# A depthwise convolution and a gated feed-forward layer on one core: the convolution's band built in four groups, the first feature block taken chunk by chunk, the last projection evicted in three parts

## The chip, the cores and the metric

The kernel runs on one core of a Trainium2 chip. The core's engines run side by side, each through its own queue in order: TensorE (PE, matmuls; its weight loads are a row of their own, PEld), VectorE (DVE), ScalarE (ACT), GpSimd (POOL) and SyncE (SP). They wait for each other through semaphores. Transfers go through 16 DMA engines, and are issued from the queues of SP, ACT or POOL. The metric is the device time of one execution in microseconds (us), the median over runs: 775.72 us before the change (three runs, 775.3 to 775.95).

## The reference

Eight sequences of 4096 tokens with 192 features go through a causal depthwise convolution of 7 taps, whose weights are a softmax over the taps and belong to 8 heads of 24 features. Its output, 32768 tokens, goes through a feed-forward layer of 1536 features with a ReLU gate.

```python
w = weight - np.max(weight, axis=-1, keepdims=True)
w = np.exp(w)
w = w / (np.sum(w, axis=-1, keepdims=True) + 1e-09)
x_pad = np.concatenate([np.zeros((B, pad, D), dtype=np.float32), x], axis=1)
idx = np.arange(S)[:, None] + np.arange(K)[None, :]
x_unf = x_pad[:, idx, :].reshape(B, S, K, H, group)
out = np.einsum('hk,bskhg->bshg', w, x_unf)
...
gate = np.maximum(x @ w_gate, 0.0)
val = x @ w_val
return (gate * val @ w_out).astype(np.float32)
```

Inputs and output are float32; the kernel computes its matmuls on float16 operands.

## The kernel before

**Units.** The work is cut into 16 units of 1024 tokens (`UNIT`) of two sequences at a time, four sequences apart. Features lie on partitions in three chunks of 64 (`NCH`); the two sequences take the lower and the upper 64 partitions of one tile, so that two matmuls with 64 rows run side by side. `Wg` and `Wv` are loaded into the lower half by GpSimd's queue and copied into the upper half, columns in five pieces (`CUTS`, 128, 256, 384, 384 and 384 columns); DVE copies the first two pieces, GpSimd the rest (L164).

**One unit.** `gate_val` runs twice (windows of 512 tokens), each with 12 blocks of 128 gate features. A block is six matmuls with `Wg` into one tile of PSUM and six with `Wv` into another (L441), a ReLU on ACT (L451, it reads the gate tile) and a product on DVE (L452, it reads the value tile). PSUM is a pool of four such tiles used in rotation, so a block's value tile is needed again by the value matmuls two blocks later. Then `project` runs four times (window by sequence): 48 matmuls with `Wo` in four quarters of 128 tokens (L459), one ACT copy of 768 columns into `out_s` (L467), and one store of 384 KB issued by SP. There are three `out_s` buffers.

**Convolution.** From unit 2 on it is done elementwise for the unit after the next: ACT, DVE and GpSimd share the products and sums per tap (`lane_first`, `lane_rest`, `product`, `add`), on x that was turned round by transposing transfers. For units 0 and 1 there is no time for this, and TensorE does it: a matmul with a band matrix, 118 rows (112 tokens and 6 before them) by 112 columns, for each head. `conv_dense(0)` and `conv_dense(1)` make window 0 and window 1 of unit 0, each 120 small matmuls (L274) in three channel chunks, each chunk followed by a cast into `xc` (chunk 1 on DVE, the others on ACT, L284). `conv_dense(0)` stands before the first gate block, `conv_dense(1)` after eight blocks. `conv(2)` and `conv(3)` make unit 1, during unit 0's projection.

**The opening.** Before the band exists, the tap weights come in (L110), replicated over 64 partitions in each half: four heads on partitions 0 to 63, four on 64 to 127. DVE and ACT make the softmax (L179 to L188). GpSimd makes `eye`, an identity pattern of 64 rows in each half (L137). DVE multiplies it with the taps (`prod`, L220: 4 heads x 32 columns x 7 taps = 896 elements a partition) and sums over the taps (`blk`, L228). The result holds a 64 by 32 block of each head's band. Copies on DVE (L237, six) and ACT (L239, four) put it at its places in the two band tiles, which were zeroed. Meanwhile TensorE runs 18 matmuls on zeros (L125), and three more after `conv_dense(0)` (L478). GpSimd's queue in the opening: x loads for `conv_dense(0)`, the two selections for `eye`, eight weight loads, x loads for `conv_dense(1)`, weight copies and loads, `late` and the x loads for `conv(2)`, weight copies.

**Order.** The order on each engine is written out by hand (`manual_schedule`); a queue does not overtake. In units 0 to 13 ACT's products for the unit after the next stand ahead of the four projections, in groups of four. In unit 0 only eleven of them do, and the three for the last tap run in unit 1, ahead of blocks 4, 8 and 12 of its 24.

Of the kernel before, what the change touches and what calls it, by code (L numbers as in the profile page):

```python
# [8 lines left out]
FP = mybir.dt.float32  # L9
F16 = mybir.dt.float16  # L10
# [5 lines left out]
def kernel(  # L16
# [12 lines left out]
    nc = tc.nc  # L29

    B, S, D = x.shape
    H, KW = weight.shape
    G = D // H
    DFF = moe_w_gate.shape[1]
    PAD = KW - 1
    NB = B // 2
    NCH = D // 64
    NBLK = D // 32
    NFF = DFF // 128
    WIN = 512  # L40
    NWIN = S // WIN
    SUB = 112
# [8 lines left out]
    NUNIT = NB * S // UNIT  # L51
# [9 lines left out]
    const = ctx.enter_context(tc.tile_pool(name="const", bufs=1))  # L61
# [42 lines left out]
    xts = {}  # L104
    xts[0] = load_x(0)

    HH = H // 2
    wr = const.tile([128, HH, KW], FP)
    for half, eng in ((0, nc.sync), (1, nc.scalar)):
        eng.dma_start(  # L110
            out=wr[64 * half : 64 * half + 64],
            in_=bass.AP(
                tensor=weight.tensor,
                offset=weight.offset + half * HH * KW,
                ap=[[0, 64], [KW, HH], [1, KW]],
            ),
        )
    ones = const.tile([128, 32 + KW], FP)
    nc.vector.memset(ones[:], 1.0)

    zeros = const.tile([128, 512], F16)
    nc.vector.memset(zeros[:], 0.0)  # L122
    ps = psum.tile([128, 2, 512], FP, name="ps")
    for n in range(18):
        nc.tensor.matmul(  # L125
            out=ps[:, n % 2, :], lhsT=zeros[:, 0:128], rhs=zeros[:], start=True, stop=True
        )

    bands = [const.tile([128, HH, SUB], F16, name=f"band{half}") for half in range(2)]
    for half in range(2):  # L130
        nc.vector.memset(bands[half][:], 0.0)

    eye = const.tile([128, 32 + KW], FP)
    for half in range(2):
        nc.gpsimd.affine_select(  # L137
            out=eye[64 * half : 64 * half + 64],
            in_=ones[64 * half : 64 * half + 64],
            pattern=[[-1, 32 + KW]],  # L140
            compare_op=ALU.is_equal,
            fill=0.0,
            base=0,
            channel_multiplier=1,
        )

# [42 lines left out]
            out=e[:], in0=e[:], in1=sm[:].to_broadcast([128, n, KW]), op=ALU.mult  # L189
        )  # L190

    we = const.tile([128, HH, KW], FP)
    softmax(we, wr, HH)

    tap = const.tile([128, NCH, KW], FP)

    def load_taps():
        late = const.tile([128, HH, KW], FP)
        nc.gpsimd.tensor_copy(out=late[:], in_=we[:])
        for c in range(NCH):  # L200
            r0 = 0
            while r0 < 64:
                h = (64 * c + r0) // G
                r1 = min(64, G * (h + 1) - 64 * c)
                for half in range(2):
                    p0 = 64 * (h // HH)
                    nc.sync.dma_start(
                        out=tap[64 * half + r0 : 64 * half + r1, c, :],
                        in_=late[p0 : p0 + r1 - r0, h % HH, :],
                    )  # L210
                r0 = r1

# [1 line left out]
    xts[2] = load_x(2)  # L214
    pool_halves(4)

    prod = const.tile([128, HH, 32, KW], FP)
    e0 = eye[:, 0:1]
    w0 = we[:, 0:1, 0:1]
    nc.vector.tensor_tensor(  # L220
        out=prod[:],
        in0=bass.AP(tensor=e0.tensor, offset=e0.offset, ap=[e0.ap[0], [0, HH], [1, 32], [1, KW]]),
        in1=bass.AP(tensor=w0.tensor, offset=w0.offset, ap=[w0.ap[0], [KW, HH], [0, 32], [1, KW]]),
        op=ALU.mult,
    )
    blk = const.tile([128, HH, 32, 1], F16)
    with nc.allow_low_precision("one of the terms is not zero"):
        nc.vector.tensor_reduce(out=blk[:], in_=prod[:], axis=mybir.AxisListType.X, op=ALU.add)  # L228

    places = [(0, 0, 64, 0), (64, 0, 64, 64), (32, 0, 32, 32), (64, 32, 64, 32), (96, 0, 32, 96)]  # L230
    for half in range(2):
        for n, (r0, b0, b1, s0) in enumerate(places):
            ncol = min(32, SUB - s0)
            src = blk[64 * half + b0 : 64 * half + b1, :, 0:ncol, 0]
            dst = bands[half][r0 : r0 + b1 - b0, :, s0 : s0 + ncol]
            if n % 2 == 0:
                nc.vector.tensor_copy(out=dst, in_=src)  # L237
            else:
                nc.scalar.copy(out=dst, in_=src)  # L239

    def band(h):
        return bands[h // HH][0 : SUB + PAD, h % HH, :]

    xc = {}

# [138 lines left out]
    def product(engine, u, c, k):  # L384
        out = prods[u][:, k, c, :]
        in_, scale = shifted(u, c, k, 1), tap[:, c, k : k + 1]
        if engine is nc.scalar:
            engine.activation(out=out, in_=in_, func=ACTF.Copy, scale=scale)  # L388
        else:
            engine.tensor_scalar(out=out, in0=in_, scalar1=scale, scalar2=None, op0=ALU.mult)  # L390
# [37 lines left out]
    def gate_val(u, w):  # L428
        h = hpool.tile([128, NFF, 2, WIN], F16, name="hT")
        xcb = xc[u]  # L430
        for f in range(NFF):
            if u == 0 and w == 0 and f == 8:
                conv_dense(1)
            if u == 1 and w * NFF + f in (4, 8, 12):
                product(nc.scalar, u + 1, (w * NFF + f) // 4 - 1, KW - 1)
            pss = []
            for W in (Wg, Wv):
                ps = psum.tile([128, 2, 512], FP, name="ps")
                for c in range(NCH):
                    for st in range(2):  # L440
                        nc.tensor.matmul(  # L441
                            out=ps[:, st, :],
                            lhsT=W[64 * st : 64 * st + 64, c, 128 * f : 128 * (f + 1)],
                            rhs=xcb[64 * st : 64 * st + 64, c, WIN * w : WIN * (w + 1)],
                            start=(c == 0),
                            stop=(c == NCH - 1),
                            tile_position=(64 * st, 0),
                        )
                pss.append(ps)
            gr = gpool.tile([128, 2, WIN], F16, name="gr")  # L450
            nc.scalar.activation(out=gr[:], in_=pss[0][:], func=ACTF.Relu)  # L451
            nc.vector.tensor_tensor(out=h[:, f], in0=gr[:], in1=pss[1][:], op=ALU.mult)  # L452
        return h

    def project(bp, w, h, st):
        ps = psum.tile([128, 2, 512], FP, name="ps")
        for q in range(4):
            for f in range(NFF):
                nc.tensor.matmul(  # L459
                    out=ps[:, q // 2, D * (q % 2) : D * (q % 2) + D],  # L460
                    lhsT=h[:, f, st, 128 * q : 128 * (q + 1)],
                    rhs=Wo[:, f, :],
                    start=(f == 0),
                    stop=(f == NFF - 1),
                )
        os_ = opool.tile([128, 2, 2 * D], FP, name="out_s")
        nc.scalar.copy(out=os_[:], in_=ps[:, :, 0 : 2 * D])  # L467
        row0 = (bp + NB * st) * S + WIN * w
        nc.sync.dma_start(
            out=out[row0 : row0 + WIN, :].rearrange("(q p) d -> p q d", p=128),  # L470
            in_=os_[:].rearrange("p a (b d) -> p (a b) d", d=D),
        )


    conv_dense(0)
    ps = psum.tile([128, 2, 512], FP, name="ps")
    for n in range(3):
        nc.tensor.matmul(  # L478
            out=ps[:, n % 2, :], lhsT=zeros[:, 0:128], rhs=zeros[:], start=True, stop=True
        )  # L480
    lane_load(2)
    nc.gpsimd.dma_start(out=Wo[:], in_=moe_w_out.rearrange("(c p) d -> p c d", p=128))
    for u in range(NUNIT):
        lane = 1 <= u < NUNIT - 1
        if lane:
            add(u + 1, 1)
        if u == 1:
            lane_load(3)
            add(2, 2)
            add(2, 3)  # L490
        if u + 2 < NUNIT:
            lane_turn(u + 2)
        if u == 0:
            xts[3] = load_x(3)
        if 0 < u < NUNIT - 3:
            lane_load(u + 3)
        if lane:
            for k in range(4 if u == 1 else 2, KW - 1):
                add(u + 1, k)
        hs = [gate_val(u, w) for w in range(2)]  # L500
        if lane:
            add(u + 1, KW - 1)
        if u == 0:
            xc[1] = xcpool.tile([128, NCH, UNIT], F16, name="xc")
            conv(2)
        del xc[u]
        work = [[] for _ in range(4)]
        if u + 2 < NUNIT:
            lane_first(u + 2)
            lane_rest(u + 2)  # L510
            todo = [(c, k) for k in (0, 1, 2, 3, 4, 6) for c in range(NCH)]
            todo = [ck for ck in todo if ck not in VECTOR[u > 0] and (u or ck[1] < 6)]
            work = [todo[4 * i : 4 * i + 4] for i in range(4)]
        bp, w0 = u * UNIT // S, u * UNIT % S // WIN
        for i in range(4):
            for c, k in work[i]:
                product(nc.scalar, u + 2, c, k)
            project(bp, w0 + i // 2, hs[i // 2], i % 2)
            if u == 0 and i == 0:
                conv(3)  # L520

# [29 lines left out]
```

## Time and profile before

| what | us |
|---|---|
| median of three runs | 775.72 (775.3 to 775.95) |
| the profiled execution | 776.04 |
| its span on the core | 774.3 |
| TensorE matmuls busy | 767.1 (99%) |
| VectorE busy | 687.1 (89%) |
| ScalarE busy | 602.4 (78%) |
| GpSimd busy | 371.4 (48%) |
| first gate matmul starts | 10.86 |
| last projection matmul ends, by the chain | 769.80 |

The span is one profiled execution, from its first instruction to its last; the execution's own time is 1.7 us longer. The granted clock of TensorE is 1.0 throughout. Busy times of matmuls overlap, as they are pipelined; the chain of waits, followed back from the last instruction, says better what sets the end. Per block of gate and value work TensorE takes 1.295 us, per projection 4.0 us.

### The profile page before, as it was taken

The page shows a single profiled execution, that of the slowest core. Times are in us where ns is not written, and L with a number is a line of the kernel's source. Part 1 is how long each engine was busy: PE and PEld are TensorE (multiplying, and loading weights), DVE is VectorE, ACT ScalarE, POOL GpSimd, SP SyncE. Part 2 cuts the span into 40 slices and gives each one's busy share as a digit, 9 for nine tenths or more (in the row PEclk, how much of TensorE's full clock was granted, in tenths as well). Part 3 has the DMA queues.
Part 4 walks back from the last instruction along what each step waited for, and adds up shares of the span by engine and source line. Part 5 has one row for each costly group of instructions (what it writes and reads, how often), then busy time and mean ns, then how long its engine had stood idle before and what let it go on. Part 6 is the DMA issues. An engine that isn't in the chain of part 4 may idle for free.

```text
span 774.3 us, 19017 instructions
## 1 busy us (share of the span) xinstructions
PE 767.1 (99%) x7957; PEld 501.5 (65%) x7957; DVE 687.1 (89%) x733; ACT 602.4 (78%) x732; POOL 371.4 (48%) x213
## 2 busy tenths in 40 slices
PE   9999999999999999999999999999999999999997
PEld 4485584856748466484765848567484674847657
DVE  7889999989999899999999999899998999995590
ACT  5797887878778887787878878788787877875571
POOL 9606829084380935709266291743909346080000
PEclk9999999999999999999999999999999999999999
DMA  9957828171272813628153281622828021200102
GB/s 114 129 96 125 90 83 93 42 115 20 88 88 63 105 28 80 75 79 98 31 94 52 83 91 41 106 30 83 92 63 106 22 80 37 67 18 22 62 2 82
DMA packets 132565, 55.63 MB, mean 72 GB/s; under 512 B 98176, under 2 KB 132480, under 8 KB 132480
## 3 DMA queue, kind: packets, MB, share of 16 engines
q1 hardware_dynamic: 90592, 38.45, 24.3%
q0 software_dynamic: 41808, 15.97, 18.8%
q8 instruction: 62, 1.02, 0.6%
q14 instruction: 23, 0.19, 0.1%
q10 hardware_dynamic: 80, 0.01, 0.0%
HBM read 31.94 MB, written 25.17 MB: 74 GB/s over the span
## 4 chain that ended last, share of the span: by engine, by line
PE 98%; DVE 1%; DMA 0%; issue 0%; ACT 0%; DVEq 0%; ACTq 0%
PE ps L441 65%; PE ps L459 33%; PE ps L274 0%; DMA wr<-in_weight_dram 0%; PE ps L299 0%; DVE prod L220 0%; DVE blk L228 0%; ACT out_s L467 0%; PE ps L478 0%; DVE band L237 0%; ACT we L183 0%; DVE we L188 0%; DVE we L180 0%; DVE sm L185 0%; DVE mx L179 0%
## 5 line engine op out<-in xcount | busy, mean ns | idle before, releaser
L452 DVE TENSOR_TENSOR hT<-gr,ps 128x1024 f16<-128x1024 f16 x384 | 468.6, 1221 | 62.9 <-ACT gr L451 36.5
L451 ACT ACTIVATE gr<-ps 128x1024 f16<-128x1024 f32 x384 | 393.3, 1024 | 99.5 <-PE ps L441 99.2
L394 POOL TENSOR_TENSOR prods<-prods 128x1344 f32<-128x1344 f32 x70 | 212.3, 3033 | 313.5 <-DVE prods L390 288.0
L441 PE MATMUL ps<-xc,Wg 64*128 64x512 f16 x2304 | 311.9, 376 | 0.0
L441 PE MATMUL ps<-xc,Wv 64*128 64x512 f16 x2304 | 311.7, 376 | 0.0
L459 PEld LDWEIGHTS <-hT 128*128 128x128 f16 x3072 | 252.7, 98 | 6.4 <-issue 6.4
L459 PE MATMUL ps<-Wo,hT 128*128 128x192 f16 x3072 | 256.4, 246 | 0.0
L441 PEld LDWEIGHTS <-Wv 64*128 64x128 f16 x2304 | 130.1, 94 | 118.9 <-issue 0.8
L441 PEld LDWEIGHTS <-Wg 64*128 64x128 f16 x2304 | 111.5, 94 | 134.6 <-issue 2.8
L417 DVE SCALAR_TENSOR_TENSOR acc<-x_r,tap,acc 128x576 f32<-128x576 f16 x210 | 154.3, 812 | 1.7 <-ACT acc L405 1.7
L388 ACT ACTIVATE prods<-x_r,tap 128x448 f32<-128x448 f16 x222 | 130.4, 662 | 0.0
L467 ACT COPY out_s<-ps 128x768 f32<-128x768 f32 x64 | 50.9, 796 | 60.1 <-PE ps L459 44.7
L350 POOL DMA_DIRECT2D x_e<-in_x_dram x56 | 45.1, 816 | 3.5 <-POOL x_p L369 2.4
L369 POOL COPY x_p<-x_e 128x1728 f16<-128x1728 f16 x28 | 44.7, 1625 | 3.8 <-DMA x_e<-in_x_dram 3.8
L394 POOL TENSOR_TENSOR xc<-prods 128x1344 f16<-128x1344 f32 x14 | 42.4, 3027 | 1.1
L417 DVE SCALAR_TENSOR_TENSOR xc<-x_r,tap,acc 128x576 f16<-128x576 f16 x42 | 31.8, 812 | 0.0
L405 ACT ACTIVATE acc<-x_r,tap 128x576 f32<-128x576 f16 x42 | 29.4, 765 | 0.0
L390 DVE TENSOR_SCALAR prods<-x_r,tap 128x448 f32<-128x448 f16 x72 | 27.3, 450 | 0.0
L125 PE MATMUL ps<-zeros 128*128 128x512 f16 x18 | 6.7, 555 | 1.5 <-DVE zeros L122 1.5
L92 POOL DMA_DIRECT2D x_h<-in_x_dram x8 | 6.7, 843 | 0.8 <-POOLq L535 0.8
L125 PEld LDWEIGHTS <-zeros 128*128 128x128 f16 x18 | 2.3, 135 | 5.4 <-issue 3.5
L274 PE MATMUL ps<-band,x_h 118*32 118x112 f16 (+7 forms) x240 | 3.4, 209 | 1.2 <-issue 0.8
(41 smaller groups left out, 47.9 us busy)
## 6 DMA issues: line engine op xcount, KB each, us to landing
out_dram<-out_s SPq DMA_DIRECT2D x64, 384.0 KB
x_e<-in_x_dram POOLq DMA_DIRECT2D x34, 192.0 KB, 5.8
x_e<-in_x_dram POOLq DMA_DIRECT2D x22, 240.0 KB, 5.3
x_r<-x_p SPq DMA_TRANSPOSE x126
x_h<-in_x_dram POOLq DMA_DIRECT2D x4, 240.0 KB, 5.8
x_h<-in_x_dram POOLq DMA_DIRECT2D x4, 192.0 KB, 4.3
Wo<-in_moe_w_out_dram POOLq DMA_DIRECT2D x1, 576.0 KB, 9.5
Wg<-in_moe_w_gate_dram POOLq DMA_DIRECT2D x3, 144.0 KB, 4.1
```

The source lines that it names most:

```text
L350: nc.gpsimd.dma_start(out=xe[:, j : j + n, st, :, :].rearrange("p j c r -> p j (c r)"), in_=bass.AP(tensor=x.tensor, offset=x.offset + (b ...
L369: nc.gpsimd.tensor_copy(out=xp[:, :, :, st, :], in_=xe[:, :, st, :, :])
L388: engine.activation(out=out, in_=in_, func=ACTF.Copy, scale=scale)
L390: engine.tensor_scalar(out=out, in0=in_, scalar1=scale, scalar2=None, op0=ALU.mult)
L394: nc.gpsimd.tensor_tensor(out=pr[:, 0] if k < KW - 1 else xc[u][:, :, LDVE:UNIT], in0=pr[:, 0], in1=pr[:, k], op=ALU.add,)
L405: nc.scalar.activation(out=accs[u][:, c, :], in_=shifted(u, c, 0, 0), func=ACTF.Copy, scale=tap[:, c, 0:1],)
L417: nc.vector.scalar_tensor_tensor(out=xc[u][:, c, 0:LDVE] if k == KW - 1 else acc[:, c, :], in0=shifted(u, c, k, 0), scalar=tap[:, c, k : k ...
L441: nc.tensor.matmul(out=ps[:, st, :], lhsT=W[64 * st : 64 * st + 64, c, 128 * f : 128 * (f + 1)], rhs=xcb[64 * st : 64 * st + 64, c, WIN * ...
L451: nc.scalar.activation(out=gr[:], in_=pss[0][:], func=ACTF.Relu)
L452: nc.vector.tensor_tensor(out=h[:, f], in0=gr[:], in1=pss[1][:], op=ALU.mult)
L459: nc.tensor.matmul(out=ps[:, q // 2, D * (q % 2) : D * (q % 2) + D], lhsT=h[:, f, st, 128 * q : 128 * (q + 1)], rhs=Wo[:, f, :], start=(f ...
L467: nc.scalar.copy(out=os_[:], in_=ps[:, :, 0 : 2 * D])
```

## The change

The band of each head is now built from a block of 32 rows and 38 columns, in four groups of 32 partitions with two heads each (`HQ`): the tap weights come in replicated over 32 partitions of each group, so that every softmax step, `prod` (2 x 38 x 7 = 532 elements) and `blk` work on half the heads; GpSimd makes four selections for `eye`, 44 columns wide instead of 39; sixteen copies put the blocks into the bands, four for each group, ten on DVE and six on ACT. `load_taps` reads the same values from their new partitions.

TensorE runs 16 matmuls on zeros at the start instead of 18, and none after `conv_dense(0)`. In the first block of `gate_val` the twelve matmuls go by channel chunk (gate and value of chunk 0, then of chunk 1, then of chunk 2); both of its PSUM tiles are taken at once, as in all blocks. `conv_dense(1)` stands ahead of block 7 instead of block 8. The three products of the last tap for unit 2 stand with the others in unit 0 (groups of 4, 4, 4 and 2). The very last projection is split: its first two quarters, its third and its fourth each have a PSUM tile, a copy (ACT, DVE, ACT) and a store (issued by SP, SP, ACT).

```diff
-    HH = H // 2
-    wr = const.tile([128, HH, KW], FP)
+    HQ = H // 4
+    wr = const.tile([128, HQ, KW], FP)
     for half, eng in ((0, nc.sync), (1, nc.scalar)):
...
-                offset=weight.offset + half * HH * KW,
-                ap=[[0, 64], [KW, HH], [1, KW]],
+                offset=weight.offset + 2 * half * HQ * KW,
+                ap=[[HQ * KW, 2], [0, 32], [1, HQ * KW]],
...
-    ones = const.tile([128, 32 + KW], FP)
+    BW = 32 + PAD
+    ones = const.tile([128, BW + PAD], FP)
...
-    for n in range(18):
+    for n in range(16):
...
-    for half in range(2):
+    for q in range(4):
         nc.gpsimd.affine_select(
-            out=eye[64 * half : 64 * half + 64],
-            in_=ones[64 * half : 64 * half + 64],
-            pattern=[[-1, 32 + KW]],
+            out=eye[32 * q : 32 * q + 32],
+            in_=ones[32 * q : 32 * q + 32],
+            pattern=[[-1, BW + PAD]],
...
-            base=0,
+            base=PAD,
...
-    prod = const.tile([128, HH, 32, KW], FP)
+    prod = const.tile([128, HQ, BW, KW], FP)
...
-    blk = const.tile([128, HH, 32, 1], F16)
+    blk = const.tile([128, HQ, BW, 1], F16)
...
-    places = [(0, 0, 64, 0), (64, 0, 64, 64), (32, 0, 32, 32), (64, 32, 64, 32), (96, 0, 32, 96)]
-    for half in range(2):
-        for n, (r0, b0, b1, s0) in enumerate(places):
-            ncol = min(32, SUB - s0)
-            src = blk[64 * half + b0 : 64 * half + b1, :, 0:ncol, 0]
-            dst = bands[half][r0 : r0 + b1 - b0, :, s0 : s0 + ncol]
-            if n % 2 == 0:
+    for q in range(4):
+        for j in range(4):
+            s0 = 32 * j - PAD
+            lo, hi = max(0, -s0), min(BW, SUB - s0)
+            rows = min(32, SUB + PAD - 32 * j)
+            src = blk[32 * q : 32 * q + rows, :, lo:hi, 0]
+            h0 = q % 2 * HQ
+            dst = bands[q // 2][32 * j : 32 * j + rows, h0 : h0 + HQ, s0 + lo : s0 + hi]
+            if j < 2 or (j == 2 and q % 2 == 0):
                 nc.vector.tensor_copy(out=dst, in_=src)
             else:
                 nc.scalar.copy(out=dst, in_=src)
...
-            if u == 0 and w == 0 and f == 8:
+            if u == 0 and w == 0 and f == 7:
                 conv_dense(1)
-            if u == 1 and w * NFF + f in (4, 8, 12):
-                product(nc.scalar, u + 1, (w * NFF + f) // 4 - 1, KW - 1)
...
+            pss = [psum.tile([128, 2, 512], FP, name="ps") for _ in range(2)]
+            order = [(i, c) for i in range(2) for c in range(NCH)]
+            if u == 0 and w == 0 and f == 0:
+                order.sort(key=lambda ic: ic[1])
+            for i, c in order:
+                W = (Wg, Wv)[i]
...
-    def project(bp, w, h, st):
+    def project(bp, w, h, st, final):
+        parts = [range(4)] if not final else [range(2), range(2, 3), range(3, 4)]
         row0 = (bp + NB * st) * S + WIN * w
+        for n, qs in enumerate(parts):
+            ps = psum.tile([128, 2, 512], FP, name="ps")
...
+            os_ = opool.tile([128, 2, 2 * D], FP, name="out_s")
+            k = len(qs)
+            a, m = (k + 1) // 2, min(k, 2) * D
+            copy = nc.vector.tensor_copy if n == 1 else nc.scalar.copy
+            copy(out=os_[:, 0:a, 0:m], in_=ps[:, 0:a, 0:m])
+            (nc.scalar if n == 2 else nc.sync).dma_start(
...
     conv_dense(0)
-    ps = psum.tile([128, 2, 512], FP, name="ps")
-    for n in range(3):
-        nc.tensor.matmul(
-            out=ps[:, n % 2, :], lhsT=zeros[:, 0:128], rhs=zeros[:], start=True, stop=True
-        )
...
-            todo = [ck for ck in todo if ck not in VECTOR[u > 0] and (u or ck[1] < 6)]
+            todo = [ck for ck in todo if ck not in VECTOR[u > 0]]
...
-            project(bp, w0 + i // 2, hs[i // 2], i % 2)
+            project(bp, w0 + i // 2, hs[i // 2], i % 2, u == NUNIT - 1 and i == 3)
```

More of the change, by code (lines that the diff above doesn't have):

```diff
@@ L127 @@
         )
-    bands = [const.tile([128, HH, SUB], F16, name=f"band{half}") for half in range(2)]
+    bands = [const.tile([128, 2 * HQ, SUB], F16, name=f"band{half}") for half in range(2)]
     for half in range(2):
         nc.vector.memset(bands[half][:], 0.0)
-    eye = const.tile([128, 32 + KW], FP)
-    for half in range(2):
+    eye = const.tile([128, BW + PAD], FP)
+    for q in range(4):
         nc.gpsimd.affine_select(
-            out=eye[64 * half : 64 * half + 64],
-            in_=ones[64 * half : 64 * half + 64],
-            pattern=[[-1, 32 + KW]],
+            out=eye[32 * q : 32 * q + 32],
+            in_=ones[32 * q : 32 * q + 32],
+            pattern=[[-1, BW + PAD]],
             compare_op=ALU.is_equal,
             fill=0.0,
-            base=0,
+            base=PAD,
             channel_multiplier=1,
@@ L190, in softmax @@
         )
-    we = const.tile([128, HH, KW], FP)
-    softmax(we, wr, HH)
+    we = const.tile([128, HQ, KW], FP)
+    softmax(we, wr, HQ)
     tap = const.tile([128, NCH, KW], FP)
     def load_taps():
-        late = const.tile([128, HH, KW], FP)
+        late = const.tile([128, HQ, KW], FP)
         nc.gpsimd.tensor_copy(out=late[:], in_=we[:])
@@ L205, in load_taps @@
                 for half in range(2):
-                    p0 = 64 * (h // HH)
+                    p0 = 32 * (h // HQ)
                     nc.sync.dma_start(
                         out=tap[64 * half + r0 : 64 * half + r1, c, :],
-                        in_=late[p0 : p0 + r1 - r0, h % HH, :],
+                        in_=late[p0 : p0 + r1 - r0, h % HQ, :],
                     )
@@ L221 @@
         out=prod[:],
-        in0=bass.AP(tensor=e0.tensor, offset=e0.offset, ap=[e0.ap[0], [0, HH], [1, 32], [1, KW]]),
-        in1=bass.AP(tensor=w0.tensor, offset=w0.offset, ap=[w0.ap[0], [KW, HH], [0, 32], [1, KW]]),
+        in0=bass.AP(tensor=e0.tensor, offset=e0.offset, ap=[e0.ap[0], [0, HQ], [1, BW], [1, KW]]),
+        in1=bass.AP(tensor=w0.tensor, offset=w0.offset, ap=[w0.ap[0], [KW, HQ], [0, BW], [1, KW]]),
         op=ALU.mult,
     )
-    blk = const.tile([128, HH, 32, 1], F16)
+    blk = const.tile([128, HQ, BW, 1], F16)
     with nc.allow_low_precision("one of the terms is not zero"):
         nc.vector.tensor_reduce(out=blk[:], in_=prod[:], axis=mybir.AxisListType.X, op=ALU.add)
-    places = [(0, 0, 64, 0), (64, 0, 64, 64), (32, 0, 32, 32), (64, 32, 64, 32), (96, 0, 32, 96)]
-    for half in range(2):
-        for n, (r0, b0, b1, s0) in enumerate(places):
-            ncol = min(32, SUB - s0)
-            src = blk[64 * half + b0 : 64 * half + b1, :, 0:ncol, 0]
-            dst = bands[half][r0 : r0 + b1 - b0, :, s0 : s0 + ncol]
-            if n % 2 == 0:
+    for q in range(4):
[7 more added lines that the diff above has]
+            if j < 2 or (j == 2 and q % 2 == 0):
                 nc.vector.tensor_copy(out=dst, in_=src)
@@ L241, in band @@
     def band(h):
-        return bands[h // HH][0 : SUB + PAD, h % HH, :]
+        return bands[h // (2 * HQ)][0 : SUB + PAD, h % (2 * HQ), :]
     xc = {}
@@ L431, in gate_val @@
         for f in range(NFF):
-            if u == 0 and w == 0 and f == 8:
+            if u == 0 and w == 0 and f == 7:
                 conv_dense(1)
-            if u == 1 and w * NFF + f in (4, 8, 12):
-                product(nc.scalar, u + 1, (w * NFF + f) // 4 - 1, KW - 1)
-            pss = []
-            for W in (Wg, Wv):
-                ps = psum.tile([128, 2, 512], FP, name="ps")
[L439 to L447, printed above, removed]
-                        )
-                pss.append(ps)
+            pss = [psum.tile([128, 2, 512], FP, name="ps") for _ in range(2)]
[4 more added lines that the diff above has]
+                W = (Wg, Wv)[i]
+                for st in range(2):
+                    nc.tensor.matmul(
+                        out=pss[i][:, st, :],
+                        lhsT=W[64 * st : 64 * st + 64, c, 128 * f : 128 * (f + 1)],
+                        rhs=xcb[64 * st : 64 * st + 64, c, WIN * w : WIN * (w + 1)],
+                        start=(c == 0),
+                        stop=(c == NCH - 1),
+                        tile_position=(64 * st, 0),
+                    )
             gr = gpool.tile([128, 2, WIN], F16, name="gr")
@@ L453, in gate_val @@
         return h
-    def project(bp, w, h, st):
[L456 to L467, printed above, removed]
-        row0 = (bp + NB * st) * S + WIN * w
[L469 to L472, printed above, removed]
@@ L475 @@
-    conv_dense(0)
-    ps = psum.tile([128, 2, 512], FP, name="ps")
-    for n in range(3):
-        nc.tensor.matmul(
-            out=ps[:, n % 2, :], lhsT=zeros[:, 0:128], rhs=zeros[:], start=True, stop=True
-        )
+    def project(bp, w, h, st, final):
+        parts = [range(4)] if not final else [range(2), range(2, 3), range(3, 4)]
+        row0 = (bp + NB * st) * S + WIN * w
+        for n, qs in enumerate(parts):
+            ps = psum.tile([128, 2, 512], FP, name="ps")
+            for i, q in enumerate(qs):
+                for f in range(NFF):
+                    nc.tensor.matmul(
+                        out=ps[:, i // 2, D * (i % 2) : D * (i % 2) + D],
+                        lhsT=h[:, f, st, 128 * q : 128 * (q + 1)],
+                        rhs=Wo[:, f, :],
+                        start=(f == 0),
+                        stop=(f == NFF - 1),
+                    )
+            os_ = opool.tile([128, 2, 2 * D], FP, name="out_s")
[4 more added lines that the diff above has]
+            (nc.scalar if n == 2 else nc.sync).dma_start(
+                out=out[row0 + 128 * qs[0] : row0 + 128 * (qs[0] + k), :].rearrange(
+                    "(q p) d -> p q d", p=128
+                ),
+                in_=os_[:, 0:a, 0:m].rearrange("p a (b d) -> p (a b) d", d=D)
+                if k == 4
+                else os_[:, 0, 0:m].rearrange("p (b d) -> p b d", d=D),
+            )
```

## The prediction

> **What bounds the kernel now.** I read the page first, then the chain of waits in order of time, then the rows by shape for the opening, then the DMA queues and the windows around the two ends.
>
> ```profile
> span 774.3 us, 19017 instructions
> PE 767.1 (99%) x7957; PEld 501.5 (65%) x7957; DVE 687.1 (89%) x733; ACT 602.4 (78%) x732; POOL 371.4 (48%) x213
> PE 98%; DVE 1%; DMA 0%; issue 0%; ACT 0%; DVEq 0%; ACTq 0%
> ```
>
> TensorE is the bound: 98% of the chain is matmuls, and their number in the main loop (4608 gate and value, 3072 projection) does not change. A change can win only where the chain is not a necessary matmul. The chain from the start shows those places (start us, length us, what):
>
> ```profile
> 5.45 1.10 DVE prod L220
> 6.57 1.10 DVE blk L228
> ...
> 8.09 0.34 DVE band L237
> 8.43 0.14 issue
> 8.56 1.61 PE ps L274 x112
> 10.18 0.75 PE ps L478 x3
> 10.93 10.47 PE ps L441 x96
> 21.40 1.48 PE ps L274 x114
> 22.88 0.80 issue
> 23.68 0.23 PE ps L274 x3
> ```
>
> Before the first gate matmul lie a DVE chain, the first convolution and three matmuls on zeros (L478). Inside the second convolution TensorE stands 0.80 us with nothing to wait for that the profile shows. The third place is unit 1, whose 288 chain steps of gate and value work take longer than those of the next unit:
>
> ```profile
> 62.41 31.58 PE ps L441 x288
> 109.93 31.19 PE ps L441 x288
> ```
>
> The fourth is the end. TensorE ends at 769.80; the windows after it (stretch, its length, busy us by engine, clock, DMA share, GB/s) show one ACT copy, 0.8 us until packets flow, packets, and the closing:
>
> ```profile
> 769.80:770.70 0.90, 0.00 (x0) 0.00 (x0) 0.00 (x0) 0.80 (x1) 0.00 (x0) 1.00 0.00 0
> 770.70:771.50 0.80, 0.00 (x0) 0.00 (x0) 0.00 (x0) 0.00 (x0) 0.00 (x0) 1.00 0.00 0
> 771.50:772.90 1.40, 0.00 (x0) 0.00 (x0) 0.00 (x0) 0.00 (x0) 0.00 (x0) 1.00 0.89 280
> 772.90:774.30 1.40, 0.00 (x0) 0.00 (x0) 0.00 (x0) 0.00 (x0) 0.00 (x0) 1.00 0.00 1
> ```
>
> **Opening, DVE chain.** The five softmax steps on 28 elements take 14; I take 0.07 us off, from about 1 ns an element. `prod` and `blk` shrink from 896 to 532 elements. Both last 1.09 us; with some 0.15 us fixed (the 128x4 steps of the softmax take 0.17 to 0.18) that is 1.05 ns an element, so each loses 0.38. The copies into the band then start at 7.69 - 0.83 = 6.86, say 6.90. GpSimd makes four selections instead of two, 0.31 us apart; the last ends near 5.35, just before `prod` at 5.40.
>
> **The copies** go from ten to sixteen, ten on DVE, six on ACT, each of at most 76 elements instead of 128.
>
> ```profile
> L237 DVE COPY band<-blk 32x128 f16<-32x128 f16 x2 | 0.4, 184 | 0.0
> L237 DVE COPY band<-blk 32x64 f16<-32x64 f16 x2 | 0.5, 257 | 0.0
> L239 ACT COPY band<-blk 32x128 f16<-32x128 f16 x2 | 0.6, 295 | 0.0
> ```
>
> Half the elements are no cheaper, so I take 0.20 us a copy on DVE and 0.31 on ACT (their spacing). Until now the convolution waited for three DVE copies. Its second matmul now needs a head of the second group, so five DVE copies (6.90 + 1.00) and three on ACT (6.90 + 0.93). With the 0.13 us from copy to matmul seen before, it runs from about 8.05 instead of 8.56. The sixteen zeros end at 7.62, since the last two of eighteen started at 7.62 and 7.83. The third channel block needs all ten copies, 8.90 + 0.11, about 0.1 later than TensorE wants it. The convolution has issued at 9.57 instead of 9.98.
>
> **First gate block.** Without the zeros it follows 0.13 us later, as the zeros did: 9.70 instead of 10.86. Behind the ten copies DVE still makes two weight copies (0.21 spacing), then the cast of the second chunk (0.69): 8.94 to 9.42, 9.45 to 10.14. ACT casts chunk 0 by 9.36, chunk 2 by 10.41. Chunk by chunk, four matmuls take 0.43 us; those of chunk 1 wait from 10.13 to 10.25. The block ends at 11.11 instead of 12.17, 1.06 earlier. But its order delays the gate's last matmul by almost half a block: the Relu can start only at 10.90 + 0.21, instead of at half the block. Relu 1.02, product 1.22 and 0.1 to TensorE give 13.45, when the buffer of the first value tile is free for the third block's value matmuls. They started at 14.11. So 0.40 of 1.06 goes into a new wait, **0.66 us** stays. Bounds: 0.9 (no late cast) to 0.2 (DVE copies at 0.25).
>
> GpSimd's queue behind the two more selections is 0.5 us later: all weight and x loads and three pairs of weight copies. Who waits: DVE's weight copies have 0.9 us of cover (first gate weights landed at 4.63 + 2.9 = 7.53), the fourth block's weights come at 13.1 and 14.2 for 14.10 and 14.75, later ones have about 1 us. Nothing is added; without cover the price is at most 0.5.
>
> **The 0.80 us stall.** The page counts 62 instruction packets of 1.02 MB for 7957 matmuls with their loads, 257 instructions each. The stall falls after 18+120+3+96+114 = 351 matmuls, 702 instructions. The boundary before it is at 446, 14 matmuls ahead of this convolution, about 19.8. Among the queues between 21.4 and 21.5 us a packet of that kind starts:
>
> ```profile
> q8 instruction: 1, 0.02, 60.1%
> ```
>
> It takes 0.96 us and TensorE resumes 2.2 us after its start. I read this as TensorE running out of instructions, since 240 of them pass in 1.6 us. Counted through the whole trace in the same way, packets start 0.1 to 1.5 us before their boundary while the DMA engines are idle, and up to 2 us (once 3.6) after it while loads run. Here x loads issued at 17.35 and 18.28 flowed from 18.7 on. In the changed kernel five matmuls are gone and the convolution comes one block earlier, at about 19.28. The boundary falls on its fourth matmul, the next one 11 matmuls behind it, at 22.05. The x loads flow only from 19.2, and the packet, usually 0.5 ahead of its boundary, starts at 18.8: instructions come at 21.0, no stall. What then ends the wait is the product of the block before: DVE was done with it at 22.98, and the next gate matmuls (23.85) can't be much before 23.07. Gain **0.78 us**. Unknown; the other end is a packet 3.6 late: 19.3 + 3.6 + 2.2 = 25.1, a stall of 3.0 and a loss of 2.2. I take the good end, as this packet is ahead of the loads, but narrowly.
>
> [...]
>
> **Three products moved.** In unit 1 ACT ran one (0.66 us) before the gate blocks 4, 8 and 12; TensorE slipped three times 0.13, the 31.58 against 31.19. Gain **0.38 us** (0.25 if part has another cause). They now stand in ACT's queue in unit 0's projection, one before the third `out_s` copy, two before the fourth. There ACT sat idle 2.92 us before that copy, and three at 0.57 spacing are 1.7. Without that cover, up to 1.7 us on the copy. DVE and GpSimd users of these products come a unit later.
>
> **The end.** The last ACT copy has 192 columns instead of 768. From 0.80 us for 768 and 0.59 for 512 I get 0.82 ns a column and 0.32 for 192: 0.48 less. Its store is 96 KB instead of 384; 1.27 us of packets become 0.32: 0.95 less. The store's issue and the 1.4 us behind the last packet stay. The first part's store (192 KB) flows near 769.2 to 769.9, the second's near 770.1 to 770.4, the last from 771.1: no collision. The last copy's buffer was that of the third half, whose packets ended at 768.9. The added DVE copy lies a whole quarter (1.0 us) ahead of the end, the last store in ACT's queue has nothing behind it. Sum 1.43; **1.43 us**, bounds 1.0 (half of the packet term) to 1.6.
>
> [...]
>
> **Sum:** 0.66 + 0.78 + 0.38 + 1.43 = 3.25 us. The profiled execution took 776.04, span 774.3 and 1.7 around it; it gives 772.8. The median of the runs is 0.32 below it, 775.72, so 772.5.
>
> **Rivals.**
> - *The fetch stall stays or grows.* For it: the packet clears the loads by only 0.4 us. With the old 3.85 us from boundary to resumption: 19.3 + 3.85 = 23.15 against 22.05, 1.1 us instead of 0.80. Instead of 0.78 gained, 0.3 lost: 775.72 - 2.17 = 773.6.
> - *DVE's ten copies become the opening's bound.* One copy of six took 0.33 us. Were all so, the tenth would end 1.3 us later, and the 0.66 becomes -0.6: 773.7. Against: the other five took 0.19.
> - *The clock falls back, ending slower.* Place: the opening, where zeros kept TensorE busy, and the next convolution. The first twelve zeros came every 0.427 us, from 6.97 on every 0.216: 5.45 us at half rate. Each such stretch costs half, 2.7; two give 775.72 - 3.25 + 5.45 = 777.9. It decides from 6.5 us at half rate. Against: after the gaps of 0.35 and 0.80 us the matmuls kept full pace, and no new gap is over 0.45.
>
> **Chances.** Forecast 0.60 (own range 771.7 to 773.2), fetch stall 0.20, copies 0.10, fetch and copies together 0.05 (774.8), clock 0.05. The range, 771.6 to 774.2, reaches over both single rivals with some of their unknowns. About 0.2%, 1.55 us, can be told from no change: faster 0.88, within it 0.07 (both rivals together and a worse fetch), slower 0.05.
>
> **What would show it.** Copies starting near 6.9; the first gate matmul near 9.7, without zeros; a TensorE wait on DVE near 13.4; no idle time within or just behind the second convolution; 31.2 us for unit 1's gate work; 3.1 us from TensorE's last matmul to the end instead of 4.5. An idle stretch of TensorE near 22 us, or matmuls at 0.43 us after 8 us, would make it wrong.

## The result, and the profile after

The changed kernel is a little slower: 776.75 us (median of 20 runs, 776.42 to 777.37) against 775.70 us before; the ratio is 1.0015, 95% interval 1.0008 to 1.0022. The forecast was 772.5, faster.

The profiled execution took 776.87 us (776.04 before), its span is 774.5 (774.3), so the time around the span grew from 1.70 to 2.37. In the trace the end itself did what was forecast, and the three moved products too. The opening and the second convolution did not. The chain of waits of the changed kernel from the start (start us, length us, what):

```profile
0.83 4.26 DMA wr<-in_weight_dram
...
5.19 0.18 DVE mx L180
...
6.73 0.72 DVE prod L221
...
7.48 0.72 DVE blk L229
...
8.22 0.17 DVE band L240
...
9.39 1.72 PE ps L277 x104
...
11.13 0.70 DVE xc L287
...
15.07 5.37 PE ps L444 x48
...
22.79 1.45 PE ps L444 x11
24.24 1.27 issue
25.51 21.11 PE ps L444 x193
```

Read the first line first, beside the same two lines of the kernel before:

```profile
0.83 2.90 DMA wr<-in_weight_dram
...
3.83 0.19 DVE mx L179
```

Before, the load of the tap weights lasted from 0.83 to 3.73 and the softmax began at 3.83; now the load lasts until 5.09 and the softmax begins at 5.19, 1.36 us later. From there on the DVE chain is as short as forecast (the copies begin 3.03 us behind the softmax, 3.86 before), yet they begin at 8.22 instead of 7.69. The second line to read is the last idle one: 11 matmuls behind the second convolution TensorE runs into an idle stretch of 1.27 us, where the forecast had none. Unit 1 starts at 64.21 instead of 62.34.

The end, in the chain of the same kernel:

```profile
755.55 15.96 PE ps L464 x192
771.51 0.03 ACTq L475
771.54 0.04 issue
771.58 0.32 ACT out_s L475
```

TensorE ends at 771.51, 1.71 us later than before, and the span 3.0 us after that instead of 4.5: the shorter copy and store are there.

Where did the load's 1.36 us come from? The DMA queues between 1.9 and 5.2 us, before:

```profile
q0 software_dynamic: 728, 0.27, 81.3%
q1 hardware_dynamic: 80, 0.01, 1.6%
q10 hardware_dynamic: 80, 0.01, 1.6%
```

and after:

```profile
q0 software_dynamic: 299, 0.11, 57.1%
q1 hardware_dynamic: 66, 0.00, 1.0%
q10 hardware_dynamic: 66, 0.00, 1.0%
```

q1 and q10 carry nothing but the two tap loads there, 64 rows each. What comes on top of 64 are packets of 4 bytes: 16 before, 2 after. The load is half as many bytes, in rows of 56 instead of 112; the x loads on q0 move 299 packets in that stretch instead of 728. The delay is in one of the two loads. ACT's, on q10, has its last packet at 2.86 us (2.81 before). SP's, on q1, starts its first packet only then (before, at 2.47, while the other still ran), as if it stood behind the other, and has its last at 4.79 instead of 3.42.

The old pattern was 64 by 28; the new one is 2 by 32 by 14. With the outer dimension of two came 2 packets of 4 bytes in place of 16, and the later landing; e1, e2 and e4 show that it is the cause. On how many DMA engines a load ran no row shows: the two engines of theory A in e1 are the author's reading of the 2 packets.

### The profile page after: what moved, and what is told of

The parts are those of the page before. It is cut to its first block, busy times and chain, and to the rows that moved or that the text cites. A ratio compares the mean times of both kernels' runs of the same rounds, so it can differ in the third digit from the quotient of the medians.

```text
span 774.5 us, 19025 instructions
## 1 busy us (share of the span) xinstructions
PE 765.4 (99%) x7952; PEld 505.7 (65%) x7952; DVE 688.0 (89%) x738; ACT 602.3 (78%) x735; POOL 371.8 (48%) x215
## 4 chain that ended last, share of the span: by engine, by line
PE 97%; DVE 1%; ACT 1%; DMA 1%; issue 1%; ACTq 0%; DVEq 0%
PE ps L444 64%; PE ps L464 33%; DMA wr<-in_weight_dram 1%; DVE hT L454 0%; ACT gr L453 0%; PE ps L302 0%; PE ps L277 0%; ACT prods L391 0%; DVE band L240 0%; DVE prod L221 0%; DVE blk L229 0%; DVE xc L287 0%; ACT out_s L475 0%; ACT we L184 0%; DVE we L181 0%
## 5 line engine op out<-in xcount | busy, mean ns | idle before, releaser
L444 PEld LDWEIGHTS <-Wv 64*128 64x128 f16 x2304 | 132.0, 94 | 119.2 <-issue 2.9
L444 PEld LDWEIGHTS <-Wg 64*128 64x128 f16 x2304 | 115.2, 94 | 131.6 <-issue 3.1
L475 ACT COPY out_s<-ps 128x768 f32<-128x768 f32 (+1 forms) x65 | 50.8, 782 | 58.3 <-PE ps L464 44.2
L126 PE MATMUL ps<-zeros 128*128 128x512 f16 x16 | 5.0, 482 | 1.5 <-DVE zeros L123 1.5
```

The lines of the kernel that those rows point to most:

```text
L444: nc.tensor.matmul(out=pss[i][:, st, :], lhsT=W[64 * st : 64 * st + 64, c, 128 * f : 128 * (f + 1)], rhs=xcb[64 * st : 64 * st + 64, c, WI ...
L475: copy(out=os_[:, 0:a, 0:m], in_=ps[:, 0:a, 0:m])
```

## The experiments

Each run was timed beside the kernel before on the same chip (medians of that kernel there: 775.31 to 775.36). In the expectations, theory A is that of the load and of an instruction packet held up by x loads. An instruction packet is one of the 62 transfers of 16 KB on q8, which the profile names "instruction". By the author's estimate each brings TensorE its next 257 instructions (7957 matmuls, each with its weight load, over 62); a boundary is the matmul at which, so counted, one packet's instructions end.

**e1: the load without its outer dimension.** Against the changed kernel; the bands of half the heads are filled from other heads' taps.

```diff
-                ap=[[HQ * KW, 2], [0, 32], [1, HQ * KW]],
+                ap=[[0, 64], [KW, HQ], [1, KW]],
```

> The changed kernel with its two tap loads read as 64 rows of 14 elements, without the outer dimension of two; heads 0 and 1 then stand on all of partitions 0 to 63, heads 4 and 5 on 64 to 127, so the bands of the other heads are filled from these. Theory A: the loads were late (softmax at 5.19 instead of 3.83) because with an outer dimension of two their 64 packets run on two DMA engines only, beside the x loads. Then the load lands near 3.8, the band copies start near 6.9, the first gate matmul near 9.7, and the time falls by at least 1.3 us, 776.75 to 775.4; and if the instruction packet then lies ahead of the x loads, as the prediction had it, the 1.27 us stall goes too: 774.2 or less. Theory B: the loads are late because of their 56-byte packets or by accident of the x loads: softmax stays near 5.1 and the time near 776.7.

Measured: 774.23 us, 2.5 less than the changed kernel. Softmax at 3.83, copies at 6.87, first gate matmul at 9.59, as the prediction had them (6.90 and 9.70). The loads have 80 packets again, 16 beside the 64 rows:

```profile
q1 hardware_dynamic: 80, 0.00, 1.3%
```

The stall behind the second convolution was still 1.11 us in the profiled execution, which took 775.05 us, 0.8 more than the median: its instruction packet came at 21.27, among the x loads.

**e2: the outer dimension alone, in the kernel before.**

```diff
-                ap=[[0, 64], [KW, HH], [1, KW]],
+                ap=[[0, 2], [0, 32], [1, HH * KW]],
```

> The kernel before, with one part of the change alone: its two tap loads get an outer dimension of two (the same 28 elements to the same partitions). Theory A: the softmax starts near 5.2 instead of 3.83, and the chain up to the first gate matmul moves by 1.3 us: time 775.7 + 1.3 = 777.0, more or less as the instruction packet falls. Theory B: softmax at 3.8, time 775.7.

Measured: 777.22 us against 775.33, ratio 1.0029 (1.0020 to 1.0037). The chain of this kernel:

```profile
0.82 4.28 DMA wr<-in_weight_dram
...
24.36 0.11 issue
```

The softmax starts at 5.20 (the last line is the stall in the second convolution, 0.11 us here), with the old 112-byte rows (q1 and q10 have 66 packets each); so it is neither the smaller rows nor anything else of the change. The first gate matmul is 1.49 us later. Six of the ten runs lie at 776.83 to 777.23, four at 778.6 to 778.8; even the fastest is 1.5 us slower than the kernel before. So this one pattern costs more than the whole change lost.

**e3: the changed kernel with late x loads.**

```diff
-    xts[2] = load_x(2)
     pool_halves(4)
+    xts[2] = load_x(2)
```

> The changed kernel with the x loads for conv(2) issued behind the last pair of weight copies on GpSimd's queue, some 2.3 us later. Theory A (the stall behind the second convolution is an instruction packet held up by these loads): the packet starts before 21.5 instead of at 23.1, the stall of 1.27 us goes, the time falls by 1.1 to 1.3 us, to 775.5. Theory C (the stall has nothing to do with the loads, 256 instructions of which 240 are small simply pass too fast): the stall stays over 0.8 us, time 776.5 or more.

Measured: 775.31 us, 1.4 less than the changed kernel. The instruction packet starts at 21.62 instead of 23.12, and the chain runs on behind the second convolution without a gap:

```profile
22.75 0.04 issue
22.79 22.25 PE ps L444 x204
```

So the idle stretch is the wait for a packet, and these loads held it up. The packet was 0.1 us later than expected, but the next boundary lay far enough behind: at about 24.2 (22.79 and the 1.45 us of 11 matmuls), 2.6 us after the packet's start. In the changed kernel TensorE went on 2.39 us after it (23.12 to 25.51).

**e4: the taps in four loads** of 32 rows, on SP's and ACT's queues in turn, with the right heads.

```diff
-    for half, eng in ((0, nc.sync), (1, nc.scalar)):
+    for q, eng in ((0, nc.sync), (2, nc.scalar), (1, nc.sync), (3, nc.scalar)):
         eng.dma_start(
-            out=wr[64 * half : 64 * half + 64],
+            out=wr[32 * q : 32 * q + 32],
...
-                offset=weight.offset + 2 * half * HQ * KW,
-                ap=[[HQ * KW, 2], [0, 32], [1, HQ * KW]],
+                offset=weight.offset + q * HQ * KW,
+                ap=[[0, 32], [KW, HQ], [1, KW]],
```

> The changed kernel with the taps in four loads of 32 partitions (two on SP's queue, two on ACT's), no outer dimension of two, correct heads. Theory A: softmax near 4.4 (the second issue of each queue 0.6 us behind the first), band copies near 7.4, 0.8 us earlier than in the changed kernel; time 776.0 or, if the stall behind the second convolution shrinks too, down to 774.7. Theory B: softmax stays near 5.1, time 776.7.

Measured: 773.70 us against 775.33, ratio 0.9977 (0.9968 to 0.9987), 3.05 us less than the changed kernel. The softmax starts at 3.72, earlier than expected and than before; q10 has 96 packets for its two loads of 32 rows, 16 beside the rows of each. The fourth block starts at 14.10, exactly where the prediction had it, and the instruction packet at 19.76, ahead of most of the x loads, leaves 0.2 us of idle time.

**e5: the kernel before with the last projection in three parts alone** (the diff is that of `project` in the change).

> The kernel before with the last projection half in three parts, and nothing else of the change. By the prediction the time from TensorE's last matmul to the end of the span falls by 1.43 us (4.79 to 3.36 counted from that matmul's start). Theory D: this is all gained, time 775.5 - 1.4 = 774.1. Theory E: the closing around the span, which was 1.70 us before and 2.37 in the changed kernel, e1 and e3, belongs to the split and takes 0.67 back: 774.8.

Measured: 773.74 us against 775.33, ratio 0.9976 (0.9967 to 0.9985). From the last matmul's start to the end of the span it is 3.25 instead of 4.79 us: 1.54, a little more than the 1.43 forecast. Around the span it stays 1.70. Theory E falls: the longer closing is not the split's.

**e6: the kernel before with late x loads** (the edit of e3).

> The kernel before with the x loads for conv(2) issued behind the last pair of weight copies on GpSimd's queue, and nothing else. Theory A (the 0.80 us in the second convolution are an instruction packet held up by these loads): the packet starts near 19.5 instead of 21.5, the 0.80 us go, the time falls by 0.7 to 0.8 us, to 774.7. Theory C (240 small instructions simply pass too fast for any fetch): the idle stretch stays, time 775.5.

Measured: 775.30 us against 775.33: no difference in the median. But the profiled execution took 775.30 instead of 776.04; the packet starts at 19.59, and the chain has no idle stretch in the second convolution:

```profile
10.92 9.84 PE ps L441 x90
...
23.07 0.04 issue
23.11 20.90 PE ps L441 x192
```

The spread of the runs fits both. Of the kernel before, the fastest runs lie at 775.29. Of its 90 runs beside the experiments 56 lie within 0.1 of that, of the 20 beside the changed kernel only 6; the others are at 775.4 to 777.1, but for two far above. With late x loads, ten of eleven lie at 775.29 to 775.36. So the 0.80 us of the profiled execution are a wait for a packet, as theory A has it, but many executions do not have it: 0.74 is the difference between the profiled one (776.04) and the fastest. The profiles of e9 and e10 below show such executions. There the kernel before has a few tiny instructions more and its x loads in their old place; the packet starts at 19.02 and 19.99 instead of 21.48, there is no idle stretch, and unit 1 starts at 61.61 and 61.60 instead of 62.34.

**e7: both repairs in the changed kernel** (e4 and e3).

> The changed kernel with both repairs: taps in four loads without an outer dimension of two, and the x loads for conv(2) behind the last weight copies. In e4 0.2 us of TensorE's time were still lost behind the second convolution. Theory A: no idle time there, 0.2 us less than e4, near 773.4. If the packet had been early for another reason than the loads, the time is e4's 773.7 or more.

Measured: 773.31 us against 775.33, ratio 0.9974 (0.9964 to 0.9984); the fourth block at 14.08, no idle stretch behind the second convolution, unit 1 at 60.95 instead of 62.34.

**e9, e10: the closing**, the time around the span. The kernel before with eight more memsets on DVE, or five more copies on ACT, of one element a partition, early where these engines wait anyway.

```diff
+    spare = const.tile([128, 8], FP)
+    for n in range(8):
+        nc.vector.memset(spare[:, n : n + 1], 0.0)
```

> The kernel before with eight more tiny memsets on DVE in the opening, where DVE sits idle for the tap weights (1.95 to 3.83 us); nothing reads them. The changed kernel has eight DVE instructions more than before, and the time around its span is 2.37 us instead of 1.70. Theory F: the closing depends on the length of DVE's program: 2.37 around the span, time 0.67 us longer. Otherwise 1.70.

> The kernel before with five more tiny copies on ACT in the opening, as many instructions as the changed kernel has more on ACT; nothing reads them. Theory G: the closing depends on the length of ACT's program: 2.37 us around the span. Otherwise 1.70.

Measured, one profiled execution each: 775.56 with a span of 773.51, and 775.49 with 773.48, so 2.05 and 2.01 us around the span instead of 1.70. Each expectation was 2.37, 0.67 more; what was found is 0.35 and 0.31 more. The two add up to the 0.67 of the changed kernel, which has both (e1, e3 and e12 too: 2.37 and 2.38). But it is not the length of the programs. With three more on ACT and four on DVE (e5, e11) it stays at 1.70, and e4, e7 and e13, which have one more on each of the two engines than the changed kernel, have 1.78 to 1.83. What sets it was not found.

**e11: the opening as before, with the other three steps** (three parts at the end, moved products, late x loads).

> The kernel before with the last projection in three parts, the three products moved into unit 0, and the x loads for conv(2) late; opening, zeros, first block's order and the place of the second convolution as before. From e5 (773.74) and e6 the sum is 775.3 - 1.56 - 0.38 = 773.4. If the new opening (with four loads) is worth its 0.66 us in time, e7 (773.31) should lie 0.66 below this; if the closing takes it back, both are equal.

Measured: 773.39 us, ratio 0.9973 (0.9963 to 0.9983), against e7's 773.31: equal. In the traces TensorE ends 0.65 us later than in e7 (last matmul at 768.42 against 767.77), as the prediction's 0.66 says, but from that matmul to the end of the execution e11 needs 4.94 us and e7 5.47: 0.12 of it around the span, 0.41 inside. There SyncE waits for the transfers' semaphores one after the other, 0.06 us each, and in e7 the last store's is the third of nine in that list, in the changed kernel, e5 and e11 the last, when all others are done.

**e12 and e13: gate first.** The first block in the old order, in the changed kernel and in that of e7.

```diff
-            if u == 0 and w == 0 and f == 0:
-                order.sort(key=lambda ic: ic[1])
```

> The changed kernel with the first block in the old order, all gate matmuls ahead of all value matmuls, nothing else undone. The prediction's step: chunk by chunk, the Relu starts late and the third block's value matmuls wait on DVE (the third block took 1.68 us instead of 1.30). Undone, that wait goes and the fourth block starts 0.1 to 0.2 us earlier than 15.71. Rival: the old order waits for the casts at its first matmuls, and the fourth block starts 0.3 us later or more.

> The changed kernel with all that the runs so far found: taps in four loads without an outer dimension of two, the x loads for conv(2) late, and the first block in the old order (gate first). e12 against the changed kernel had the fourth block 0.55 us earlier, 0.15 of it from an earlier start of the convolution. Expected: fourth block near 13.7 instead of 14.08, time 0.4 us less than e7's 773.31, near 772.9; if the order's cost was that run's alone, 773.3.

Measured: e12 776.45 us, the fourth block at 15.16 instead of 15.71, more than the 0.1 to 0.2 us expected. TensorE's matmuls in the first three blocks of the changed kernel:

```profile
11.23 0.38 PE L444 MATMUL ps<-xc,Wv 64*128 64x512 f16 x2
11.88 0.39 PE L444 MATMUL ps<-xc,Wg 64*128 64x512 f16 x2 [0.27 <-DVE xc L287]
...
14.03 0.92 PE L444 MATMUL ps<-xc,Wg 64*128 64x512 f16 x6
15.07 0.82 PE L444 MATMUL ps<-xc,Wv 64*128 64x512 f16 x6
```

The block waits for the cast of chunk 1, and the third block's value matmuls begin 1.04 us behind its gate matmuls instead of 0.65: the wait on DVE's product that the prediction named. In e12 these follow each other at 0.65. In e13 the fourth block starts at 13.92 instead of 14.08, and unit 1 at 60.91 instead of 60.95; the time, 773.65 us (773.02 to 774.91), can't be told from e7's. The order is worth 0.16 us there, of which 0.04 are left. Of the 0.55 us in the changed kernel 0.15 are an earlier first gate matmul (10.85 instead of 11.00), which the edit doesn't explain; the rest shows only with the late opening.

## Why the prediction was wrong

**The step that failed** is "Opening, DVE chain": "The copies into the band then start at 7.69 - 0.83". It priced the shorter steps behind the load and took the load's end, 3.73, from the row of the old load; the new access pattern was costed at nothing, and not named. It cost 1.36 us (e2: 1.37 in the kernel before). Everything behind it in the opening slid: first gate matmul 11.00 instead of 9.70, fourth block 15.71 instead of 14.10. Here 0.25 us more than the 1.36 was lost, in the waits around the first block that e12 shows.

**The second step that failed** is "the packet, usually 0.5 ahead of its boundary, starts at 18.8: instructions come at 21.0, no stall". The place was right to the matmul: the stall came 11 matmuls behind the convolution. But the convolution came at 21.0 instead of 19.28, the packet fell among the x loads (start 23.12, 2.1 us behind its boundary), and 0.80 us became 1.27. It was the rival's mechanism, 1.1 us forecast there. The late opening is not the whole reason. With a timely load the convolution came at 19.36 (e1) and 19.38 (e4), near the forecast, but the packet at 21.27 and 19.76, not at 18.8, and 1.11 and 0.2 us were lost: the forecast of the packet's start was wrong by itself. Late x loads remove the stall in e3, e6 and e7, so the prediction was right to read it as a wait for instructions.

**The sum was set against the wrong time.** The gain of 0.78 was read in an execution that took 776.04, and subtracted from the median, 775.72. The runs at 775.3 had no such stall to lose (e6, and the profiles of e9 and e10). There was nothing to gain in those, and with the changed kernel's late opening there was something to lose.

**Term by term, in the profiled executions:** unit 1 starts 1.87 us later: 1.36 for the load, -0.41 for the opening's own steps up to the fourth block (forecast -0.66; -0.66 in e4 and -0.68 in e7), +0.47 for the stall (forecast -0.78), +0.21 for the wait on DVE behind the second convolution, which the old stall had covered, and 0.24 not followed further. The moved products give -0.39 in unit 1 (forecast -0.38):

```profile
64.28 31.19 PE ps L444 x288
```

TensorE's last matmul is 1.70 us later (1.87 - 0.39 + 0.22): unit 14 loses 0.22, as the value matmuls of its third block wait for DVE's product, late behind an ACT copy that came after 1.24 us of idle time without a cause in the profile. The chains of e1, e3 and e12 show the same gap there; in e4, e7 and e11 the 288 steps take 31.18 or 31.19 in every unit from 1 on. The end gives -1.54 (forecast -1.43): 0.48 from the copy (0.80 to 0.32), as forecast, and 1.06 from the store, where the prediction had 0.95. The time around the span gives +0.67, a term that the prediction kept at 1.7 without a reason; its cause is open. Together 1.70 - 1.54 + 0.67 = 0.83 = 776.87 - 776.04.

**The rivals.** The ten copies on DVE took 0.2 us each but for one of 0.36, so that rival was not it. The matmuls kept full pace: two pairs of them in the first block start 0.21 us apart (11.88 and 12.09), not 0.43. The rival that ended slower was a wrong one: what ended it there was a transfer that nobody had priced.

## What to carry to other kernels

A transfer whose access pattern changes is a changed transfer, even with fewer bytes: its landing has to be priced anew. Here an outer dimension of two moved the softmax from 3.83 to 5.19 us (5.20 in e2); 64 rows in one dimension (e1) brought it back to 3.83, four loads of 32 rows (e4) to 3.72. A gain that one profiled execution shows should be checked against the spread of the runs: if the fastest runs are faster by just that much, they probably lack the stall already. And where small matmuls passed 240 instructions in 1.6 us, x loads of 240 KB issued just ahead held up the next instructions here. Issuing them later, in e3 at 21.92 instead of 17.95 us, cost nothing and took the stall away: 1.27 us in the changed kernel (e3), 0.80 in the profiled execution of the kernel before (e6).

## What the runs showed that was not expected

- With the outer dimension of two the neighbours of the tap loads were slower too: the x loads moved 299 packets instead of 728 between 1.9 and 5.2 us (285 in e2; without it 725 in e1 and 803 in e4).
- The time around the span, 1.70 us, rose to 2.05 with eight more tiny instructions on DVE and to 2.01 with five more on ACT, while the work in the span was not longer; with nine more on DVE and six on ACT (e4, e7, e13) it was 1.78 to 1.83.
- The order in which SyncE waits at the end is worth 0.4 us: of its nine waits, 0.06 us each, six stand behind that for the last store in e4 and e7, and none in the changed kernel.
